# Output product in four strips of 160 columns, mask and memory transposes in 32-column strips, token values one segment later

## The chip, the cores and the metric

The kernel runs on one core of one Trainium2 chip. The metric is the device time of one execution in microseconds (us). An execution uses TensorE (matrix products; its weight loads are listed apart as PEld), VectorE (DVE), ScalarE (ACT), GpSimd (POOL) and the queue of SyncE (SP), which starts most transfers.

## The reference

A pre-normalised attention block with a small recurrent memory, followed by a feed-forward block, over S = 2048 tokens of width D = 640:

```python
for s in range(n_seg):                       # 64 segments of 32 tokens
    h = concat([mem, x_norm[s*32:(s+1)*32]])  # 8 memory rows + 32 token rows = 40
    q, k, v = h@Wq, h@Wk, h@Wv                # 32 heads of 128
    p = softmax(where(mask, q@k.T * scale, -1e9))
    o = (p@v) @ Wo                            # 40 x 640
    mem = o[:8]                               # the next segment's memory
    outs.append(o[8:])
h  = x + concat(outs)
h2 = h + relu(layernorm(h)@w1 + b1)**2 @ w2 + b2      # F = 1728
```

`x_norm` is the layer norm of x. A memory row sees all 40 columns; a token row sees the 8 memory columns and the tokens up to itself. All is bf16. The memory makes the 64 segments a chain: a segment's q, k and v need the output rows of the segment before.

## The kernel before, in words

**Tiling.** The order of every engine's instructions is the order of the program text (a manual schedule); a tile's buffers and the data set the waits. `step(b, sp)` handles segment s = 4b + sp; a block b is four segments, 128 tokens. The 40 rows of a segment are split in three: 8 memory rows and the first 24 token rows (a 32-row operand, `hT4`), and the last 8 token rows, the tail. The tail rows' projections do not depend on the memory, so those of four segments are gathered 32 at a time (`hTt`) and projected a block ahead, as fill work.

**TensorE in strips.** Since an operand has only 32 rows, most products use the array as four strips of 32 columns: four matmuls with different weights' columns run side by side, each writing its own 32 partitions. `proj` (L199) does q, k, v so: 5 contraction chunks * 4 strips of 512 columns for each half n of the heads. `wo_rounds` (L228), the output product, puts two halves of the heads and two halves of the 640 columns on the four strips: 16 rounds of 320 columns; the sums of the two head halves lie on different partitions and `wo_out` adds them (ScalarE copies one half, L233, VectorE adds the other, L235). `o` has 64 rows: two column halves of 320.

**A step** runs in this order on TensorE: q and k of half 0, q and k of half 1 (each evacuated by ScalarE as a row tile, then turned by VectorE, `flip`, L220; GpSimd spreads the memory queries into `qz`, L348 and L350), the memory scores `scores(0)` (L359), v half 0 and two chunks of v half 1, `scores(1)`, the mask product (L426: identity times a mask tile of 8 * 40 columns, which starts the token scores' accumulation), the token scores (L431), the rest of v. The memory rows' softmax (`soft1`, `soft2`) gives `pTm`; `values(0)` and `values(1)` (L389, L393) multiply it with `v` and with the tail values `vt4`; `values_out` (L398) copies the result into `oT`. The token rows' softmax follows on VectorE, ScalarE and GpSimd (`mxk` L439, `tk` L444, `ek` L449, `zk` L455, `rk` L457, `pk` L459, `pkt` L462). Then comes the output product of `oT[:, p, 0:32]`. Its 32 rows are the 8 memory rows of segment s and the 24 token rows of segment s - 1, since the token values of segment s (L484, L489, from `pTk` L470, `pTt` L472 and `pTx` L475) come only after it, and are copied by ScalarE at L496. From the product, `wo_out` gives `o`; `store_main` (L321) writes the token rows of s - 1, and `mem_to_hT` (L293, L297, copy L299) turns the memory rows into the next segment's `hT4`.

**Fill work.** `fill` is a list of small TensorE pieces put into fixed places of the step: 3 pieces after the token softmax's exponential, 2 before the output product, 2 before the memory transposes, the rest behind them. In blocks 1 to 14 a step has 10 pieces (the next block's tail projection: v in the first segment, q in the second, k in the third) or, in the last segment of a block, 8 pieces of the tail output product and a transpose. Blocks 0 and 15 have little or none. `late` and `mid` hold VectorE work of the layer norm at the step's start and before the output product.

**Transfers.** A block's tail values go to DRAM (`vt_d`, L310) and come back in another layout as 16 transfers (L316), four for each group g of 32 partitions. The weights of q, k, v are loaded as four chunks of 128 rows each and one chunk in two pieces of 64 rows (`load_w`, L113; `load_w4`, L118); x, the memory and copies of the mask and of `same` are issued on SP ahead of them (L125, L133, L135, L136). `ffn_biases` (L511, L513, GpSimd copy L515) loads the feed-forward bias seven segments before the end.

**Buffers** that matter: the accumulator tile `po` has one buffer of 4 banks, `chn` (scores, `pw`, `pm`) one bank, the projections three; `o` has two buffers, `v` one.

Of the kernel before, what the change touches and what calls it, by code (L numbers as in the profile page):

```python
# [9 lines left out]
ALU = mybir.AluOpType  # L10
# [6 lines left out]
def kernel(  # L17
# [16 lines left out]
    nc = tc.nc  # L34
# [22 lines left out]
    ROWS = ((0, 128), (DH, 128), (128, 128), (DH + 128, 128))  # L57
# [23 lines left out]
    selg = ident[0:64, 0:64].rearrange("p (g r) -> p g r", r=32)  # L81
    mhalf = const.tile([128, 1], F32)
    nc.vector.memset(mhalf[:], -0.5)
    mask = const.tile([128, HG, NK], BF16)
    nc.vector.memset(mask[0:32], 0.0)
    nc.gpsimd.affine_select(out=mask[0:32], in_=mask[0:32], compare_op=ALU.is_ge, fill=NEG, base=M,
                            pattern=[[0, HG], [-1, NK]], channel_multiplier=1)
# [5 lines left out]
    nc.vector.tensor_copy(out=same[0:32], in_=ident[0:32, 0:32].rearrange("p (j k) -> p j k", k=TL))  # L93
    nc.vector.tensor_reduce(out=diag[0:32], in_=same[0:32], op=ALU.add, axis=AX.X)
    nc.vector.tensor_copy(out=same[0:32], in_=diag[0:32].unsqueeze(2).to_broadcast([32, 4, TL]))
# [13 lines left out]
    def load_w(w, src):  # L109
        w2d = src.rearrange("d h e -> d (h e)")  # L110
        for c in range(4):
            r0, n = ROWS[c]
            nc.sync.dma_start(out=w[:, c * HE:(c + 1) * HE], in_=w2d[r0:r0 + n, :])  # L113

    def load_w4(w, src):
        w2d = src.rearrange("d h e -> d (h e)")
        for ch in range(2):
            (nc.scalar if ch else nc.sync).dma_start(out=w[64 * ch:64 * ch + 64, 4 * HE:5 * HE],  # L118
                                                     in_=w2d[ch * DH + 256:(ch + 1) * DH, :])
# [3 lines left out]
    def load_x(b):  # L123
        xt = s2.tile([128, D], BF16, tag="xt", name="xt")
        nc.sync.dma_start(out=xt[:], in_=x2d[b * 128:(b + 1) * 128, :])  # L125
        xts[b] = xt

    load_x(0)
    load_x(1)
    o0 = s2.tile([64, DH], BF16, tag="o", name="o")  # L130
    nc.vector.memset(o0[:], 0.0)
    for ch in range(2):
        nc.sync.dma_start(out=o0[32 * ch:32 * ch + M, :], in_=A_mem0[0][:, ch * DH:(ch + 1) * DH])  # L133
    for g in range(1, G):
        nc.sync.dma_start(out=mask[32 * g:32 * g + 32], in_=mask[0:32])  # L135
        nc.sync.dma_start(out=same[32 * g:32 * g + 32], in_=same[0:32])  # L136
    for w, src in ((wq, A_Wq), (wk, A_Wk), (wv, A_Wv)):
        load_w4(w, src)
# [26 lines left out]
    def ln_norm(b):  # L165
        mv, rs = xns[b]
        xn = s1.tile([128, D], BF16, tag="xn", name="xn")
        xt = xts.pop(b)
        for d_, s_ in ((xn[:, 0:512].rearrange("p (c g q) -> p c g q", c=2, g=2),
                        xt[:].rearrange("p (g f) -> p g f", g=2)[:, :, 0:256].rearrange("p g (c q) -> p c g q", c=2)),  # L170
                       (xn[:, 512:D].rearrange("p (g q) -> p g q", g=2),
                        xt[:].rearrange("p (g f) -> p g f", g=2)[:, :, 256:DH])):
            nc.vector.tensor_scalar(out=d_, in0=s_, scalar1=mv[:, 0:1], scalar2=rs[:, 0:1],
                                    op0=ALU.subtract, op1=ALU.mult)
        xns[b] = xn

    def ln_transpose(b):
# [5 lines left out]
        hTt = s2.tile([128, DC, 4, TL], BF16, tag="hTt", name="hTt")  # L183
        ptv = pt[:, 0:640].rearrange("p (c s t) -> p c s t", c=DC, s=4)
        nc.scalar.copy(out=hT4[:, :, :, M:SEG], in_=ptv[:, :, :, 0:HD])
        nc.scalar.copy(out=hTt[:], in_=ptv[:, :, :, HD:SEG])
# [35 lines left out]
    def wo_rounds(lhs, pw, h0, h1):  # L222
        for h in range(h0, h1):
            for kh in range(2):
                for ch in range(2):
                    j = kh * 2 + ch
# [499 lines left out]
```

## Time and profile before

| | |
|---|---|
| median of 3 runs | 1091.34 us (1088.5 to 1091.79) |
| the profiled execution | 1091.96 us |
| its span, first to last instruction | 1090.1 us |
| granted TensorE clock | 0.991 |
| TensorE busy | 1015.6 us (93%), 25284 matmuls |
| VectorE, ScalarE, GpSimd busy | 608.5, 532.3, 257.3 us (56%, 49%, 24%) |
| DMA | 38926 packets, 50.81 MB |
| first step's q product to last mask product | 63.2 to 945.8 us |
| feed-forward part | 956.3 to the end |

The span is what the trace covers; the execution's time holds 1.9 us around it. A busy TensorE is not one at its peak: its matmuls are pipelined and their ends modelled, so that times are best read from start to start. The chain that ended last is followed back from the last instruction through what released each step; what is not on it costs nothing unless its cover goes.

### The profile page before, as it was taken

The numbers are of one execution on the slowest core, as the hardware profiler recorded it, in microseconds if no ns is written. First come the engines' busy times: TensorE is split into PE (matmuls) and PEld (weight loads), VectorE is DVE, ScalarE is ACT, GpSimd is POOL, SyncE is SP. The second block draws the span as 40 slices with busy tenths as digits, with TensorE's granted clock in tenths as the row PEclk, the third lists the DMA queues.
The fourth block names the chain that finished last, engine by engine and source line by source line (L and its number), as shares of the span: only waits on it lengthen the run. The fifth ranks groups of instructions, "written<-read, shape, count | busy, mean of one in ns | idle before, by whom it ended". The sixth has DMA issues, their size and how long they took to land.

```text
span 1090.1 us, 56115 instructions
## 1 busy us (share of the span) xinstructions
PE 1015.6 (93%) x25284; PEld 559.4 (51%) x25284; DVE 608.5 (56%) x1735; ACT 532.3 (49%) x1236; POOL 257.3 (24%) x788
## 2 busy tenths in 40 slices
PE   0488999999999999999999999999999699989998
PEld 0144555555555555556555555555555355545555
DVE  1136565656565656565656565656565366555442
ACT  1035555555555555555555555555555255434332
POOL 1002222222222222222222222222222123252220
PEclk9989999999999999999999999999999899999999
DMA  8950000000000000000000000000000110332200
GB/s 227 411 184 15 12 26 13 26 13 26 13 26 13 26 13 25 14 25 13 26 14 25 14 25 14 25 14 25 14 25 8 35 30 21 117 113 73 73 25 25
DMA packets 38926, 50.81 MB, mean 47 GB/s; under 512 B 7472, under 2 KB 34080, under 8 KB 36768
## 3 DMA queue, kind: packets, MB, share of 16 engines
q1 hardware_dynamic: 38448, 45.67, 12.9%
q8 instruction: 198, 3.24, 1.3%
q10 hardware_dynamic: 240, 1.57, 0.6%
q14 instruction: 40, 0.33, 0.1%
HBM read 37.71 MB, written 9.44 MB: 43 GB/s over the span
## 4 chain that ended last, share of the span: by engine, by line
PE 86%; DMA 7%; DVE 2%; SPq 2%; ACT 1%; issue 1%; POOL 0%; DVEq 0%; POOLq 0%; ACTq 0%
PE ps L199 47%; PE pw L228 12%; PE y L679 5%; PE ps L652 5%; PE ps L228 4%; PE po L389 2%; DMA wv<-in_A_Wv_dram 2%; PE ps L431 2%; PE sm L359 2%; DMA wq<-in_A_Wq_dram 2%; PE ps L426 1%; DMA vt_d<-vt 1%; PE po L393 1%; PE pm L293 1%; PE pt L484 1%; PE pt L489 1%
## 5 line engine op out<-in xcount | busy, mean ns | idle before, releaser
L199 PEld LDWEIGHTS <-hT 128*32 128x32 bf16 x7680 | 200.4, 97 | 184.5 <-issue 9.5
L199 PE MATMUL ps<-wk,hT 128*32 128x512 bf16 x2560 | 162.0, 382 | 4.5 <-ACT vt L263 4.5
L199 PE MATMUL ps<-wv,hT 128*32 128x512 bf16 x2560 | 163.7, 383 | 0.0
L199 PE MATMUL ps<-wq,hT 128*32 128x512 bf16 x2560 | 161.6, 381 | 2.1 <-DVE hT L299 2.1
L228 PE MATMUL pw<-wo,oT 128*32 128x320 bf16 x4160 | 153.2, 299 | 1.0 <-ACT oT L496 0.7
L220 DVE STREAM_TRANSPOSE qT<-row 128x512 bf16<-128x512 bf16 x128 | 91.0, 711 | 100.5 <-ACT row L215 100.5
L215 ACT ACTIVATE row<-ps 128x512 bf16<-128x512 f32 x160 | 97.1, 607 | 85.4 <-PE ps L199 84.2
L217 ACT CAST row<-ps 128x512 bf16<-128x512 f32 x160 | 93.8, 586 | 77.1 <-PE ps L199 70.0
L228 PEld LDWEIGHTS <-oT 128*32 128x32 bf16 x4160 | 110.6, 97 | 38.3 <-ACT oT L398 0.9
L459 POOL TENSOR_TENSOR pk<-ek,rk 128x256 bf16<-128x256 bf16 x64 | 39.8, 623 | 309.0 <-DVE rk L457 191.3
L220 DVE STREAM_TRANSPOSE kT<-row 128x512 bf16<-128x512 bf16 x128 | 90.9, 710 | 19.5 <-ACT row L217 18.9
L233 ACT COPY otmp<-pw 64x320 f32<-64x320 f32 x65 | 27.5, 422 | 106.0 <-PE pw L228 106.0
L498 POOL COPY oTt<-oT 128x256 bf16<-128x256 bf16 x64 | 25.5, 398 | 217.4 <-ACT oT L496 217.4
L496 ACT CAST oT<-pt 128x512 bf16<-128x512 f32 x128 | 68.8, 593 | 4.2 <-PE pt L489 3.7
L235 DVE TENSOR_TENSOR o<-pw,otmp 64x320 bf16<-64x320 f32 x65 | 31.4, 483 | 63.2 <-ACT otmp L233 63.1
L199 PEld LDWEIGHTS <-hTt 128*32 128x32 bf16 x1920 | 37.4, 97 | 53.4 <-issue 36.6
L199 PE MATMUL ps<-wq,hTt 128*32 128x512 bf16 x640 | 48.3, 401 | 14.7 <-DMA wq<-in_A_Wq_dram 14.7
L679 PE MATMUL y<-wq,wk 128*128 128x320 bf16 x416 | 61.1, 299 | 0.1
L348 POOL COPY qz<-qT 128x96 bf16<-128x96 bf16 x126 | 33.8, 268 | 114.8 <-DVE qT L220 57.7
L368 ACT ACTIVATE em<-sm,mx 128x40 bf16<-128x40 f32 x126 | 37.5, 297 | 35.8 <-DVE mx L365 35.8
L199 PE MATMUL ps<-wv,hTt 128*32 128x512 bf16 x640 | 47.9, 398 | 6.6 <-DMA wv<-in_A_Wv_dram 6.6
L455 DVE TENSOR_REDUCE zk<-ek 128x8 f32<-128x320 bf16 x64 | 31.1, 486 | 40.0 <-ACT ek L449 40.0
(99 smaller groups left out, 1475.1 us busy)
## 6 DMA issues: line engine op xcount, KB each, us to landing
wo<-in_A_Wo_dram SPq DMA_DIRECT2D x4, 1280.0 KB
wq<-in_A_Wq_dram SPq DMA_DIRECT2D x4, 1024.0 KB
wk<-in_A_Wk_dram SPq DMA_DIRECT2D x4, 1024.0 KB
wv<-in_A_Wv_dram SPq DMA_DIRECT2D x4, 1024.0 KB
vt_d<-vt SPq DMA_DIRECT2D x16, 256.0 KB
vt<-vt_d SPq DMA_DIRECT2D x256, 16.0 KB
xt<-in_A_x_dram SPq DMA_DIRECT2D x16, 160.0 KB
out_dram<-wv SPq DMA_DIRECT2D x16, 160.0 KB
```

The lines of the kernel that those rows point to most:

```text
L199: nc.tensor.matmul(ps[32 * k:32 * k + 32, :], lhsT=lhs(c), rhs=wr[:, c, n, k], start=(c == 0), stop=(c == DC - 1))
L215: nc.scalar.mul(out=row[:], in_=ps[:], mul=scale)
L217: nc.scalar.copy(out=row[:], in_=ps[:])
L220: nc.vector.transpose(out=dst[:, n * 16:(n + 1) * 16, 0:32], in_=row[:].rearrange("p (h e) -> p h e", e=32))
L228: nc.tensor.matmul(pw[32 * j:32 * j + 32, 0:DH], lhsT=lhs(p), rhs=wo[:, head(p), ch * DH:(ch + 1) * DH], start=(h == 0), stop=(h == 15))
L235: nc.vector.tensor_tensor(out=o[:], in0=pw[0:64, 0:DH], in1=tmp[:], op=ALU.add)
L348: nc.gpsimd.tensor_copy(out=d.rearrange("p a (j f) -> p a j f", j=3)[:, :, :, 0:M], in_=src[:, :, 0:3, :])
L368: nc.scalar.activation(out=em[:], in_=sms[n][:, 0:NK], func=ACT.Exp, bias=mx[:, 0:1], scale=1.0, accum_out=zm[:])
L459: nc.gpsimd.tensor_tensor(out=pk[:], in0=ek[:, :, 0:SEG], in1=rk[:].unsqueeze(2).to_broadcast([128, HG, SEG]), op=ALU.mult)
L496: nc.scalar.copy(out=oTg[:, n, :, :, M:NK], in_=po[:, :, n * 128:(n + 1) * 128].rearrange("p g (j q) -> p g j q", q=32))
L652: nc.tensor.matmul(ps[:], lhsT=w1[:, c, fc * 128:(fc + 1) * 128], rhs=hnT[:, c, :], start=(c == 0), stop=(c == DC - 1))
L679: nc.tensor.matmul(y[:, hh, 0:DH], lhsT=f1T[:, fc, k * 128:(k + 1) * 128], rhs=w2[:, fc, cs], start=(fc == 0), stop=False, skip_group_chec ...
```

## The change

It does this, part by part:

- the output product becomes 32 rounds (one per head) of four strips of 160 columns; `o` becomes 128 rows of 160 columns with six buffers, taken out by one VectorE copy; it is stored by four transfers instead of two;
- the contraction index of x, `hT4` and the weights is permuted to match (`q c x` order), so that weights load as five chunks of 128 rows, all on SP, while x and the memory load from ScalarE's queue; the mask and `same` are computed on all partitions instead of being copied there by transfers;
- the mask product becomes four strips of 256 columns (token columns only);
- the memory transposes become 20 matmuls of 32-column shape with 8 columns each;
- the token values of segment s are computed in step s + 1, ahead of the memory values, into the same `po` tile (token columns 0 to 255, memory columns 256 to 319); the token softmax moves behind the memory values; the token rows reach the output product one segment later still, and one more output product runs at the end;
- `mid` moves behind the memory transposes;
- the tail values come back by 4 transfers instead of 16;
- `ffn_biases` moves to the first segment of block 1; the tail output of block 14 runs one segment later.

```diff
-    mask = const.tile([128, HG, NK], BF16)
-    nc.vector.memset(mask[0:32], 0.0)
+    mask = const.tile([128, HG, SEG], BF16)
+    nc.vector.memset(mask[:], 0.0)
...
-        w2d = src.rearrange("d h e -> d (h e)")
-        for c in range(4):
-            r0, n = ROWS[c]
-            nc.sync.dma_start(out=w[:, c * HE:(c + 1) * HE], in_=w2d[r0:r0 + n, :])
+        w2d = src.rearrange("(q c x) h e -> c q x (h e)", q=4, x=32)
+        for c in range(DC):
+            nc.sync.dma_start(out=w[:, c * HE:(c + 1) * HE], in_=w2d[c])
...
+    load_x(0, nc.scalar)
+    load_x(1, nc.scalar)
+    o0 = s2.tile([128, DQ], BF16, tag="o", name="o", bufs=6)
...
-    for g in range(1, G):
-        nc.sync.dma_start(out=mask[32 * g:32 * g + 32], in_=mask[0:32])
-        nc.sync.dma_start(out=same[32 * g:32 * g + 32], in_=same[0:32])
-    for w, src in ((wq, A_Wq), (wk, A_Wk), (wv, A_Wv)):
-        load_w4(w, src)
...
+    def wo_rounds(lhs, pw, p0, p1):
+        for p in range(p0, p1):
+            for q in range(4):
+                nc.tensor.matmul(pw[32 * q:32 * q + 32, 0:DQ], lhsT=lhs(p), rhs=wo[:, head(p), q * DQ:(q + 1) * DQ],
+                                 start=(p == 0), stop=(p == H - 1))
     def wo_out(pw):
-        tmp = s1.tile([64, DH], F32, tag="otmp", name="otmp")
-        nc.scalar.copy(out=tmp[:], in_=pw[64:128, 0:DH])
-        o = s2.tile([64, DH], BF16, tag="o", name="o")
-        nc.vector.tensor_tensor(out=o[:], in0=pw[0:64, 0:DH], in1=tmp[:], op=ALU.add)
+        o = s2.tile([128, DQ], BF16, tag="o", name="o", bufs=6)
+        nc.vector.tensor_copy(out=o[:], in_=pw[:, 0:DQ])
...
+        for c in range(DC):
+            for q in range(4):
+                nc.tensor.matmul(pm[32 * q:32 * q + 32, c * M:(c + 1) * M], lhsT=o[:, c * 32:(c + 1) * 32],
+                                 rhs=ident[:, 32 * q:32 * q + M], start=True, stop=True)
...
         for g in range(G):
-            for j in range(4):
-                r = 32 * g + TL * j
-                nc.sync.dma_start(out=vt4[r:r + TL].rearrange("p s u e -> p s (u e)"), in_=src[g, j])
+            nc.sync.dma_start(out=vt4[32 * g:32 * g + 32].rearrange("p s u e -> p (s u e)"), in_=src[g])
...
+    def token_values(s, v, vt4, po):
+        sp = s % 4
+        pTk, pTx = back.pop()
+        for i in range(HG):
+            for g in range(G):
+                r = slice(32 * g, 32 * g + 32)
+                nc.tensor.matmul(po[:, g, i * 32:(i + 1) * 32], lhsT=v[r, i * E:(i + 1) * E], rhs=pTk[r, i, :],
+                                 start=(i == 0), stop=False, skip_group_check=True)
...
+    def token_out(s, po):
+        for n in range(2):
+            nc.scalar.copy(out=oTg[:, n, :, :, M:NK],
+                           in_=po[:, :, n * 128:(n + 1) * 128].rearrange("p g (j q) -> p g j q", q=32))
+        nc.gpsimd.tensor_copy(out=oTts[s // 4 % 2][:, :, s % 4 * TL:(s % 4 + 1) * TL], in_=oT[:, :, 32:NK])
...
-        nc.tensor.matmul(sk[:, 0:HG * NK], lhsT=ident[:], rhs=mask[:].rearrange("p i k -> p (i k)"),
-                         start=True, stop=False, skip_group_check=True)
+        for g in range(G):
+            nc.tensor.matmul(skv[32 * g:32 * g + 32, :, M:NK], lhsT=ident[:, 0:32], rhs=mask[:],
+                             start=True, stop=False, skip_group_check=True)
...
+        nc.scalar.copy(out=v[:, 512:1024], in_=ps1[:])
+        run(fill, 3)
+        po = pop.tile([128, G, 512], F32, tag="po", name="po")
+        if s:
+            token_values(s - 1, prev["v"], prev["vt4"], po)
+        if not last:
+            for n, pT in ((0, pT0), (1, pT1)):
+                values(n, pT, po)
+                values_out(n, po)
+        run(fill, 2)
...
+        wo_rounds(lambda p: oT[:, p, 0:32], pw, 0, H)
+        if s:
+            token_out(s - 1, po)
+        o = wo_out(pw)
+        if s > 1:
+            store_main(o, s - 2)
+        if not last:
+            run(fill, 2)
+            mem_to_hT(o, hT4s[(s + 1) // 4], (s + 1) % 4)
+            tails_in((s + 1) // 4, (s + 1) % 4)
         run(mid, 2)
+        run(fill, 100)
...
-            if e == 0:
+            if (b, sp) == (1, 0):
                 ffn_biases()
...
+    po = pop.tile([128, G, 512], F32, tag="po", name="po")
+    token_values(NS - 1, prev["v"], prev["vt4"], po)
     pw = chn.tile([128, 512], F32, tag="ch", name="pw")
+    wo_rounds(lambda p: oT[:, p, 0:32], pw, 0, H)
+    token_out(NS - 1, po)
+    store_main(wo_out(pw), NS - 2)
```

## Prediction

> **What bounds the kernel now.** I read the page's chain first, then TensorE's instructions in order of time over two segments of the steady part, then the chain through the start, then the list of waits.
>
> ```profile
> PE 86%; DMA 7%; DVE 2%; SPq 2%; ACT 1%; issue 1%; POOL 0%; DVEq 0%; POOLq 0%; ACTq 0%
> ```
>
> TensorE carries 86% of the chain that ended last. The other engines matter where TensorE waits for them, and nowhere else. The second view is TensorE's own timeline: start, duration, line, tile, tile shape (contract rows * columns), count.
>
> ```profile
> 319.71 0.31 PE L426 MATMUL ps<-mask,ident 128*128 128x320 bf16 x1
> 319.95 0.38 PE L431 MATMUL ps<-kT,qT 128*32 128x40 bf16 x32
> 320.17 0.84 PE L199 MATMUL ps<-wv,hT 128*32 128x512 bf16 x12
> 320.95 0.26 PE L389 MATMUL po<-pTm,v 32*128 32x8 bf16 x16
> 321.06 0.18 PE L393 MATMUL po<-pTm,vt 32*128 32x32 bf16 x4
> 321.17 0.83 PE L199 MATMUL ps<-wk,hTt 128*32 128x512 bf16 x12
> 321.94 0.26 PE L389 MATMUL po<-pTm,v 32*128 32x8 bf16 x16
> 322.05 0.18 PE L393 MATMUL po<-pTm,vt 32*128 32x32 bf16 x4
> 322.16 0.61 PE L199 MATMUL ps<-wk,hTt 128*32 128x512 bf16 x8
> 322.60 2.35 PE L228 MATMUL pw<-wo,oT 128*32 128x320 bf16 x64
> 324.88 0.37 PE L484 MATMUL pt<-pTk,v 32*128 32x32 bf16 x32
> 325.21 0.39 PE L489 MATMUL pt<-pTx,vt 32*128 32x32 bf16 x8
> 325.53 0.61 PE L199 MATMUL ps<-wk,hTt 128*32 128x512 bf16 x8
> 326.08 0.23 PE L293 MATMUL pm<-ident,o 64*64 64x16 bf16 x4
> 326.16 0.17 PE L297 MATMUL pm<-ident,o 64*64 64x8 bf16 x2
> 326.26 0.83 PE L199 MATMUL ps<-wk,hTt 128*32 128x512 bf16 x12
> 326.92 1.25 PE L199 MATMUL ps<-wq,hT 128*32 128x512 bf16 x20
> 328.00 1.25 PE L199 MATMUL ps<-wk,hT 128*32 128x512 bf16 x20
> ...
> 348.27 0.87 PE L393 MATMUL po<-pTm,vt 32*128 32x32 bf16 x4
> ```
>
> Durations overlap, so I read starts only. Four matmuls of one tile shape run side by side; I call that a round. A 512-column round is (328.00 - 326.92) / 5 = 0.216 us. The mask product is one full-width matmul of 320 columns and takes 319.95 - 319.71 = 0.24. The output product takes 324.88 - 322.60 = 2.28 for 16 rounds of 320. Both hold a change of tile shape. With 0.10 us for such a change the output product's round is 0.136 and the mask's 0.14, which agree; so 0.10 is the price of a change of shape, and a round costs 0.0027 + 0.000417 per column (from 512 and 320). Very short rounds have a floor: 32 matmuls of 40 columns take 320.17 - 319.95 = 0.22, or 0.0275 a round, their weight loads included. From one mask product to the next (start to start) a segment lasts 13.44; 13.65 where the tail output runs, about 14.2 in the first segment of a block, about 12.6 in block 0, where no fill work exists.
>
> **Part by part.**
>
> *Mask.* Four strips of 256 columns in the shape of the products around it: one round, 0.109, against 0.24, and the change of shape ahead of it (0.10) goes too. Saved 0.23. If the four ran one after the other it would be 0.43, a loss of 0.1.
>
> *Output product.* 32 rounds of 160 columns: 32 * 0.0694 = 2.22, before 16 * 0.136 = 2.18: +0.04. No row has 160 columns; the loads are hidden at 320 and 512, and the floor of 0.0275 is under 0.069, so I take it as streaming. The far bound is stream plus a whole floor: 0.097 a round. [...] The 320-column rounds, which would have shown that at 0.16 instead of 0.136, speak against it.
>
> *Taking the product out.* ScalarE's copy (L233, 422 ns) and VectorE's sum (L235, 483 ns) become one VectorE copy of 160 columns: between L299 (40 columns, 200 ns) and L439 (320 columns, 491 ns), by straight line 0.32. From the last round's start: matmul 0.23 (by line from 40, 320 and 512 columns: 181, 299, 382 ns), copy 0.32, two handovers 0.06: 0.61. TensorE now has only two fill units to run meanwhile (0.43) plus the round itself (0.07): a new wait of 0.11, where before the token values stood there as cover. Bounds: 0 with a copy of 0.2, 0.28 with 0.49.
>
> *Memory transposes.* Before, 0.10 change of shape + 326.26 - 326.08 = 0.28. After, 20 small matmuls in the ruling shape, 5 rounds at the floor: 0.14. Saved 0.14.
>
> *Token values a segment later.* Now they open the row-tiled block ahead of the memory values. Before: three separate visits to the 32*128 shape: 321.17 - 320.95 + 0.10, 322.16 - 321.94 + 0.10, and 325.53 - 324.88 + 0.10, together 1.39; the last holds two waits of about 0.1 and 0.17 for VectorE and GpSimd (L484 to L489 is 0.33 for eight rounds of 0.0275). After: change in and out 0.2, 20 rounds at 0.0255 (between (0.22 - 0.10) / 5 = 0.024 and the floor of 0.0275), 0.51, no wait for the probabilities, which are a segment old. But memory values 1 now follow memory values 0 at once, into the same accumulator banks that ScalarE is copying out of. The trace never shows TensorE writing a bank being read. What it shows is the same two products in the first segment, when nothing covered them:
>
> ```profile
> 79.08 0.28 ACT oT L398
> ...
> 79.39 0.26 PE po L389 x16
> ```
>
> The matmul before it began at 78.87, so copy and handovers cost 0.5. The new code writes other columns of the same banks; the wait is between 0 (columns told apart) and 0.5 (the row above). I take 0.5, as the nearest row has this same pair. Behind that wait TensorE's whole queue stands, fill and output product included. [...] So 1.39 becomes 0.2 + 0.51 + 0.5 = 1.21; saved 0.18. The second copy (values_out 1) is needed only from output round 17 on, 0.43 + 1.1 later, and is hidden; uncovered it would cost 0.5.
>
> *Softmax of the tokens, moved behind the memory values.* ScalarE's ek now stands after both copies and a fill evacuation (0.59), VectorE's zk and rk end about 2.5 after the second values, the product's end comes at about 2.75 to 2.95. Hidden, narrowly; the rival below prices it. ScalarE's two token copies (1.1) and GpSimd's copies (0.4, 0.4, 0.4, then pTx 0.44) move behind the product and end some 3.2 after it; the next segment's first spread is wanted at 3.8. The layer norm, its strides included, runs behind the transposes on VectorE, off the path.
>
> Sum of a full segment: -0.23 + 0.04 + 0.11 - 0.14 - 0.18 = -0.40; and single first rounds after a change of shape cost 0.01 to 0.02 more than the rest (x8 groups: 0.44 - 0.432 etc.), some eight changes fewer: -0.12. **-0.52**, 42 segments (blocks 1 to 14, three each): **-21.8**.
>
> *First segments of a block.* L393 takes 349.06 - 348.27 = 0.79 there against 0.11 + 0.10 elsewhere in the block: each of its four matmuls has waits on the landings of four value transfers of its own. With one transfer per row group I leave 0.035 for each: 0.55 saved. 14 * (-0.52 - 0.55) = **-15.0**.
>
> *Uncovered segments* (blocks 0 and 15, seven of them, 12.6 where nothing else is in them): there the handover of 0.95 + 0.06 (copy and sum) shrinks to 0.35 and the token softmax (mxk to pTx, on the chain at 90.5 to 95.3) leaves the path. Start to start I add up 4.32 (q and k) + 0.1 + 1.51 + 0.1 + 0.11 + 0.22 + 0.65 + 0.35 + 0.13 + 0.5 + 0.23 + 2.22 + 0.6 + 0.14 + 0.42 = 11.6: -1.0 each against 12.6, and 0.35 more in the two first segments with their transfer waits: **-7.7**.
>
> *Biases.* The wait list has
>
> ```profile
> PE sm L359 <- POOL qz L348: 8.5, 1, 8.5
> ```
>
> GpSimd sat on b1f for 9.6 us until the bias landed, because SP first had to issue sixteen value loads (0.344 each from 850.94 to 856.09). That segment is 24.35 long, its neighbour 14.19. At the new place SP has four stores (0.35), one x load (0.45), the biases (1.9) and the landing (2.4) behind the output: about 6.8 after the product, plus copy and spread 0.7; TensorE asks at 5.5. Left 2.0: **-8.1**. If the wait simply moves whole, 0.
>
> *Start.*
>
> ```profile
> 15.14 16.79 DMA wq<-in_A_Wq_dram
> 31.95 21.37 DMA wv<-in_A_Wv_dram
> ```
>
> Full 128-row weight chunks land every 2.49 (TensorE's waits at 27.00, 29.50, 31.97), but SP issued the first at 13.56, after mask copies that waited for landings; the half-height pieces filled the queues until then. Now 15 chunks start at 0.72: 0.72 + about 2 + 15 * 2.49 + 0.8 for x = 40.9, against 53.3: **-12.4**. The output weights and the first value store follow in the same order, so the 4.5 wait after them moves along. Bounds: 0 (something else holds SP) to -14.
>
> *End.* One more output product, 2.2, and the token values now stand behind the last softmax and the last copy: about +3.9 from the last v to the feed-forward part; the 2.9 wait of L652 on the o buffer goes (six buffers). **+1**. Four stores instead of two per segment add 0.7 on SP, which waits for o anyway.
>
> Together -21.8 - 15.0 - 7.7 - 8.1 - 12.4 + 1 = -64.0. The profiled execution took 1091.96 (span 1090.1, 1.9 around it), 0.6 over the median of the three runs, less than the 0.3% (3 us) that can be told apart here. 1091.96 - 64.0 = **1028**.
>
> **Rivals.**
> *No bank wait.* 63 segments * 0.5 less: 1028 - 31.5 = 997. For: the columns are disjoint. Against: the row at 79.08.
> *The handover gets late.* If VectorE reaches the copy of the product only after rk, or spread falls behind GpSimd's longer tail, each 0.1 costs 6.4; a slip of 0.5 gives 1060, with half the start gain lost as well 1066. For: margins of 0.2 to 0.4. Against: VectorE is busy 56%.
> *Loads exposed (slower).* In the output product each round pays stream plus floor, 0.097 instead of 0.069: 82 products * 32 * 0.0275 = +72: 1100. It decides from 0.094 a round on, where 2624 rounds eat the 64. For: no row has so narrow a product of this kind. Against: 320-column rounds hide their loads whole.
>
> **How the numbers follow.** Forecast 0.58, its own range 1012 to 1046 (bounds of mask, copy, transposes, biases). No bank wait 0.13; late handover 0.22; exposed loads 0.06; gains cancelled to within 0.3% 0.01. The range 996 to 1060 leaves out the upper half of the late cases and the slower one. Faster 0.93, same 0.01, slower 0.06.
>
> **What would show it.** Mask to mask 12.9 in full segments and 13.1 in the first of a block; mask round 0.11; output product 2.22 plus no change of shape behind it; one gap of about 0.5 between the two memory values; a gap near 0.1 ahead of the transposes; first projections of block 0 done near 41. Wrong would be an output product over 3 us, no gap between the memory values, or a start that still ends near 53.

## The result and the profile after

The changed kernel takes **1283.53 us** (median of 4 runs, 1282.05 to 1290.51) against 1090.74 for the kernel before beside it: ratio **1.1783 [1.1736, 1.183]**. The forecast was 1028 with a range of 996 to 1060; it is wrong in size and in sign.

Three stretches of the two profiles, cut at the first and last mask product (TensorE's timeline), say where the 191.3 us of span lie:

| | before | after | difference |
|---|---|---|---|
| start to the first mask product | 76.66 | 185.66 | +109.0 |
| first to last mask product (63 segments) | 869.19 | 942.91 | +73.7 |
| last mask product to the end | 144.2 | 152.8 | +8.6 |

The chain that ended last, of the changed kernel, shares of the span by engine:

```profile
PE 76%; DMA 7%; SPq 7%; issue 7%; ACT 2%; DVE 1%; POOL 0%; DVEq 0%; POOLq 0%; ACTq 0%
```

Two entries have grown: SPq from 2% to 7% (by the page's list of lines it is L113, where SP issues the weight loads) and "issue" from 1% to 7%. "issue" is time in which TensorE waited for nothing that the profile shows. The list of TensorE's waits (us in total, times, longest) says the same by line:

```profile
PE ps L185 <- DMA wv<-in_A_Wv_dram: 50.0, 5, 12.5
...
PE pw L211 <- issue: 33.4, 42, 4.2
PE po L390 <- ACT oT L400: 28.4, 63, 0.7
```

The first row is the start; with those for wk (44.2) and wq (37.3) it makes 131.5 us, against 26.4 for the same three weights before. The last is the bank wait that the forecast priced at 0.5, in every segment. The one between is new, and so are 35 us more of "issue" on L211, L315 and L185.

**The start.** TensorE's timeline (start, duration, what, idle before):

```profile
49.13 0.62 PE L185 MATMUL ps<-wq,hTt 128*32 128x512 bf16 x4 [9.27 <-DMA wq<-in_A_Wq_dram]
```

The same wait before it ends at 39.25: a 1 MB chunk lands every 49.13 - 39.25 = 9.9 us; before, every 2.49. The transfer view for 60 to 140 us of the changed kernel (packets, MB, share of the 16 transfer engines) shows them mostly idle while TensorE waits:

```profile
q1 hardware_dynamic: 1730, 9.14, 30.9%
```

In most slices of that view the rate is 106 GB/s, a quarter of what e1 below reaches.

**The steady part.** TensorE's timeline through one output product, the counterpart of 320.95 to 326.26 before:

```profile
428.19 0.37 PE L310 MATMUL po<-pTk,v 32*128 32x32 bf16 x32
...
429.25 0.26 PE L390 MATMUL po<-pTm,v 32*128 32x8 bf16 x16 [0.43 <-ACT oT L400]
...
429.91 1.49 PE L211 MATMUL pw<-wo,oT 128*32 128x160 bf16 x75
432.09 1.14 PE L211 MATMUL pw<-wo,oT 128*32 128x160 bf16 x53 [0.69 <-issue]
433.00 0.66 PE L185 MATMUL ps<-wv,hTt 128*32 128x512 bf16 x8
433.65 0.29 PE L274 MATMUL pm<-ident,o 128*32 128x8 bf16 x20
```

The product stops after 75 of its 128 matmuls, waits for nothing, and goes on at 432.09. What TensorE lacks there is its next instructions. The trace lists their transfers as a queue of its own; its total (packets, MB, share) on the page of before, then on that of the changed kernel:

```profile
q8 instruction: 198, 3.24, 1.3%
...
q8 instruction: 248, 4.06, 1.3%
```

A packet holds 16384 bytes, and 248 of them fit TensorE's 31676 matmuls and 31684 weight loads at 256 instructions a packet (63360 / 256 = 247.5). Beside TensorE's stops, in the records of single packets:

```
packet landed   411.13   415.04   418.52   430.86
TensorE goes on 412.66   416.49   419.95   432.09
```

Over the steady part of the changed kernel 92 stops end in this way, 1.39 us (median; 1.17 to 1.60) after a packet has landed, and they sum to 77.0 us. Before there were 2, together 0.4. (The list of waits, which counts idle time alone, has 71.6 us of "issue" for the changed kernel's steady part; sums of stops here and below are good to some 6 us.) Between the stops that ended at 416.49 and 419.95 TensorE issued exactly 256 instructions. The same holds from the start of the trace on. At 77 of the 78 stops of over 0.3 us, and at all 101 in e3 below, the matmuls and loads run so far, divided by 256, give the number of packets landed so far, and in e3 the remainder falls evenly from 186 to 125. So a stop comes where TensorE has used up what has landed. In no run did two of these packets land closer together than 3.2 us (3.23 before, 3.25 in the changed kernel), so 256 / 3.2 = 80 instructions a us is the most that was ever delivered. The stretch above, to the next fill work at 433.79, has 244 matmuls with 244 loads in 433.79 - 428.19 = 5.6 us, 4.9 without the stop: 100 a us asked for. The kernel before has 178 and 178 in 5.3 us: 67.

### The profile page after: what moved, and what is told of

It is laid out like the page before. It is cut to its first block, busy times and chain, and to the rows that moved or that the text cites. A ratio compares the mean times of both kernels' runs of the same rounds, so it can differ in the third digit from the quotient of the medians.

```text
span 1281.4 us, 68779 instructions
## 1 busy us (share of the span) xinstructions
PE 1007.4 (79%) x31676; PEld 651.8 (51%) x31684; DVE 590.3 (46%) x1723; ACT 520.7 (41%) x1155; POOL 258.4 (20%) x788
## 3 DMA queue, kind: packets, MB, share of 16 engines
q1 hardware_dynamic: 41820, 46.83, 11.6%
## 4 chain that ended last, share of the span: by engine, by line
PE 76%; DMA 7%; SPq 7%; issue 7%; ACT 2%; DVE 1%; POOL 0%; DVEq 0%; POOLq 0%; ACTq 0%
PE ps L185 40%; PE pw L211 13%; SPq L113 7%; PE y L678 4%; PE ps L651 4%; DMA wv<-in_A_Wv_dram 4%; PE ps L211 3%; DMA wq<-in_A_Wq_dram 2%; PE po L390 2%; PE sm L360 2%; PE po L310 2%; ACT oT L400 1%; PE pm L274 1%; PE ps L436 1%; PE po L395 1%
## 5 line engine op out<-in xcount | busy, mean ns | idle before, releaser
L185 PEld LDWEIGHTS <-hT 128*32 128x32 bf16 x7680 | 226.0, 97 | 158.4 <-issue 11.1
L211 PE MATMUL pw<-wo,oT 128*32 128x160 bf16 x8448 | 184.7, 245 | 34.5 <-issue 33.4
L211 PEld LDWEIGHTS <-oT 128*32 128x32 bf16 x8448 | 166.5, 103 | 53.5 <-issue 45.7
L185 PE MATMUL ps<-wk,hT 128*32 128x512 bf16 x2560 | 166.0, 382 | 3.5 <-ACT vt L244 3.5
L185 PE MATMUL ps<-wq,hT 128*32 128x512 bf16 x2560 | 166.4, 383 | 2.4 <-DVE hT L276 2.3
L185 PE MATMUL ps<-wv,hT 128*32 128x512 bf16 x2560 | 163.1, 379 | 0.0
L185 PEld LDWEIGHTS <-hTt 128*32 128x32 bf16 x1920 | 47.8, 98 | 179.5 <-issue 151.7
L320 ACT CAST oT<-po 128x512 bf16<-128x512 f32 x128 | 74.9, 585 | 107.2 <-PE pw L211 102.1
L465 POOL TENSOR_TENSOR pkt<-ek,rk 128x64 bf16<-128x64 bf16 x64 | 18.9, 295 | 434.1 <-DVE rk L463 352.8
L185 PE MATMUL ps<-wq,hTt 128*32 128x512 bf16 x640 | 53.6, 406 | 47.5 <-DMA wq<-in_A_Wq_dram 37.3
L185 PE MATMUL ps<-wv,hTt 128*32 128x512 bf16 x640 | 48.4, 395 | 50.0 <-DMA wv<-in_A_Wv_dram 50.0
L349 POOL COPY qz<-qT 128x96 bf16<-128x96 bf16 x126 | 33.4, 265 | 258.2 <-DVE qT L206 184.1
L185 PE MATMUL ps<-wk,hTt 128*32 128x512 bf16 x640 | 48.0, 395 | 44.2 <-DMA wk<-in_A_Wk_dram 44.2
L400 ACT CAST oT<-po 128x128 bf16<-128x128 f32 x126 | 33.5, 266 | 89.6 <-PE po L395 89.5
L216 DVE CAST o<-pw 128x160 bf16<-128x160 f32 x66 | 21.4, 325 | 101.2 <-PE pw L211 101.2
L206 DVE STREAM_TRANSPOSE qTt<-row 128x512 bf16<-128x512 bf16 x32 | 20.6, 676 | 100.6 <-ACT row L201 100.6
L211 PE MATMUL ps<-wo,oTt 128*32 128x160 bf16 x2048 | 50.9, 236 | 14.1 <-issue 13.8
```

The costliest lines, as they stand in the source:

```text
L185: nc.tensor.matmul(ps[32 * k:32 * k + 32, :], lhsT=lhs(c), rhs=wr[:, c, n, k], start=(c == 0), stop=(c == DC - 1))
L206: nc.vector.transpose(out=dst[:, n * 16:(n + 1) * 16, 0:32], in_=row[:].rearrange("p (h e) -> p h e", e=32))
L211: nc.tensor.matmul(pw[32 * q:32 * q + 32, 0:DQ], lhsT=lhs(p), rhs=wo[:, head(p), q * DQ:(q + 1) * DQ], start=(p == 0), stop=(p == H - 1))
L320: nc.scalar.copy(out=oTg[:, n, :, :, M:NK], in_=po[:, :, n * 128:(n + 1) * 128].rearrange("p g (j q) -> p g j q", q=32))
L349: nc.gpsimd.tensor_copy(out=d.rearrange("p a (j f) -> p a j f", j=3)[:, :, :, 0:M], in_=src[:, :, 0:3, :])
L400: nc.scalar.copy(out=oTg[:, n, :, :, 0:M], in_=po[:, :, c0:c0 + 4 * M].rearrange("p g (j m) -> p g j m", m=M))
```

## The experiments

The theory: the start is lost because a weight chunk's source is now cut in four (`c q x`, outermost 4) and keeps only a share of 0.25 of the 16 transfer engines busy (62 to 134 us of the changed kernel, 106 GB/s), and the steady part because the split product needs instructions faster than they arrive. Its rival is the slower one of the prediction: the narrow rounds pay their weight loads and the new waits cost more than the parts saved. Gaps below are TensorE's stops that end 1.1 to 1.7 us after an instruction packet. "Densest 4 us" is the number of TensorE instructions in 4 us that 1% of the steady part's 4 us stretches exceed, divided by 4; it can lie above 80, by what had landed ahead. Each ratio is to the kernel before in the same batch of runs (medians 1090.74 to 1092.26); first mask, steady part, gaps and density are of the one profiled execution.

| kernel | median us | ratio to before | first mask | steady part | gaps, us | densest 4 us, per us |
|---|---|---|---|---|---|---|
| before | 1090.74 | | 76.66 | 869.19 | 0.4 | 76 |
| after | 1283.53 | 1.1783 [1.1736, 1.183] | 185.66 | 942.91 | 77.0 | 100 |
| e1 plain rows | 1158.95 | 1.0611 [1.058, 1.0643] | 65.07 | 935.82 | 72.5 | 102 |
| e4 eight pieces | 1235.44 | 1.1326 [1.127, 1.1382] | 120.45 | 956.50 | 77.1 | 100 |
| e2 half the product's instructions | 1188.73 | 1.0894 [1.0862, 1.0927] | 185.75 | 854.86 | 13.0 | 89 |
| e3 copies later | 1277.31 | 1.1709 [1.1671, 1.1747] | 186.71 | 935.09 | 102.6 | 107 |
| b1 split product on before | 1191.23 | 1.0916 [1.0881, 1.0951] | 76.65 | 964.03 | 75.7 | 100 |
| b2 as many, spread, on before | 1111.14 | 1.0185 [1.0156, 1.0214] | 76.36 | 885.89 | 13.2 | 88 |
| c2 = e1 + e2 + e3 | 1051.63 | 0.9637 [0.9614, 0.966] | 66.13 | 835.57 | 25.9 | 94 |
| v1 | 1140.07 | 1.0448 [1.042, 1.0476] | 78.29 | 908.88 | 28.3 | 95 |
| v2 | 1087.76 | 0.9948 [0.9924, 0.9972] | 65.12 | 874.79 | 32.4 | 96 |
| v3 | 1087.2 | 0.9965 [0.9953, 0.9977] | 64.90 | 874.52 | 25.9 | 95 |
| v4 | 1066.67 | 0.9771 [0.9748, 0.9794] | 65.93 | 855.18 | 3.5 | 82 |

### e1: the same chunks from plain rows

```diff
-        w2d = src.rearrange("(q c x) h e -> c q x (h e)", q=4, x=32)
+        w2d = src.rearrange("(c r) h e -> c r (h e)", r=128)
```

> The changed kernel, with the q, k and v weights loaded as five plain chunks of 128 consecutive rows (the rows' permutation is left out, so the products pair rows that do not belong together). Same bytes, same 15 transfers, same queue. Theory (the shape of the source decides the rate): in the changed kernel a chunk takes 9.55 us from landing to landing, in the kernel before 2.49; with plain rows the chunks land every 2.5 again, the first mask product comes near 70 instead of 185.7, and the time falls by 105 to 115, to about 1173. Rival (SP or the other queue holds the chunks back): the chunks still land every 9.5 and the time stays within 10 of 1283.

The first mask product comes at 65.07, 120.6 us earlier than in the changed kernel and 11.6 earlier than before. The transfer view for 20 to 40 us of this run:

```profile
DMA packets 1154, 8.41 MB, mean 421 GB/s; under 512 B 128, under 2 KB 128, under 8 KB 128
q1 hardware_dynamic: 1153, 8.40, 101.0%
```

Chunks of the same bytes, 26.42 - 23.95 = 2.47 apart by TensorE's waits, and all engines busy. The edit touches nothing else of the transfers, so the whole loss of the start is the form of the source. The time fell by 124.6, somewhat more than the 105 to 115 expected. The steady part keeps its 72.5 us of gaps: the two losses are separate.

### e4: the outer dimension eight instead of four

```diff
-        w2d = src.rearrange("(q c x) h e -> c q x (h e)", q=4, x=32)
+        w2d = src.rearrange("(q c x) h e -> c q x (h e)", q=8, x=16)
```

> The changed kernel, with the weights' 128 rows of a chunk taken as 8 pieces of 16 rows instead of 4 pieces of 32 (the pairing of the rows is then left out). Theory (a transfer of this kind keeps only as many packets in flight as its outer dimension has pieces: 4 of 16 engines busy in the changed kernel, 25%): 8 in flight, about 212 GB/s, a chunk every 4.8 us; the first mask product near 115 instead of 185.7, the time near 1212. Rival (any source in three dimensions runs at about 106 GB/s): a chunk still takes 9.5, the time stays near 1283.

The transfer view for 40 to 70 us:

```profile
DMA packets 810, 6.09 MB, mean 203 GB/s; under 512 B 44, under 2 KB 72, under 8 KB 72
q1 hardware_dynamic: 809, 6.07, 51.7%
```

TensorE's waits for chunks end at 52.74 and 57.73. Four pieces 9.9 us a chunk at 106 GB/s, eight 5.0 at 203, whole rows 2.47 at 421: from four pieces to eight the rate doubled. The busy share of the transfer engines did too: 0.25 in the changed kernel (two tenths in most slices of its view, where the last slices raise the mean to 30.9%), 51.7% here, against 101.0% with whole rows. The time, 1235.44 over two runs, misses the 1212 expected by 23 us: the first chunks took 6.0 to 6.7 us each, so that the first mask product came at 120.45 instead of 115, and the steady part was 13.6 us longer than the changed kernel's, for a reason that stays open.

### e2: half the product's instructions

```diff
-        for p in range(p0, p1):
+        for p in range(p0, p1, 2):
             for q in range(4):
-                nc.tensor.matmul(pw[32*q:32*q+32, 0:DQ], lhsT=lhs(p), rhs=wo[:, head(p), q*DQ:(q+1)*DQ], ...)
+                nc.tensor.matmul(pw[32*q:32*q+32, 0:DH], lhsT=lhs(p + q//2),
+                                 rhs=wo[:, head(p + q//2), q%2*DH:(q%2+1)*DH], ...)
```

> The changed kernel, with the output product as 16 rounds of 320 columns: the two halves of the heads land on different partitions and only 160 of each 320 columns are taken on, so the sum of the head halves is left out. The columns that TensorE streams per product are the same (16 * 320 = 32 * 160); the matmuls and weight loads are halved, 64 pairs fewer per segment and 64 fewer per tail product. Theory (TensorE runs out of instructions): the gaps that end about 1.4 us after an instruction packet has landed (92 of them, about 77 us) disappear almost wholly, and the time falls by 70 to 100, to 1185 to 1215. Rival (160-column rounds are slow by themselves, their loads exposed): rounds would be longer inside a product, not between; a product's continuous stretch is 0.069 a round already, so the gain would be under 10.

The columns streamed are the same, in 64 matmuls instead of 128. The steady part is 88.1 us shorter than the changed kernel's and its gaps shrink from 77.0 to 13.0. The timeline of the same stretch:

```profile
617.59 0.29 PE L391 MATMUL po<-pTm,v 32*128 32x8 bf16 x16
...
618.37 0.26 PE L391 MATMUL po<-pTm,v 32*128 32x8 bf16 x16 [0.43 <-ACT oT L401]
...
619.04 2.39 PE L211 MATMUL pw<-wo,oT 128*32 128x320 bf16 x64
621.21 0.65 PE L185 MATMUL ps<-wv,hTt 128*32 128x512 bf16 x8
621.84 0.29 PE L275 MATMUL pm<-ident,o 128*32 128x8 bf16 x20
```

The product is whole (621.21 - 619.04 = 2.17) and the forecast's other waits now stand free: 617.59 to 618.37 is 0.78 for a group that takes 608.15 - 607.99 = 0.16 where nothing holds it (c2), a bank wait of 0.62; 621.21 to 621.84 is 0.63 for two fill rounds of 0.43, a handover wait of 0.20. The gain of 94.8 is within the 70 to 100 expected, but the gaps did not go "almost wholly".

### e3: both copies out behind both products

```diff
-                values(n, pT, po)
-                values_out(n, po)
+                values(n, pT, po)
+            for n in range(2):
+                values_out(n, po)
```

> The changed kernel, with ScalarE's two copies of the memory values both put behind the second memory values product, so that no copy reads the accumulator banks while TensorE has still to write them. In the changed kernel TensorE waits 0.45 for the first copy in each of 63 segments. Theory (bank wait, freely additive): -28, to 1255. Theory (TensorE also short of instructions): the wait let instructions gather, so only a part comes back: -8 to -22, with the gaps after instruction packets growing by the rest. Rival (the wait was for something else, such as the probabilities of half 1): no change, and the gap between the two products stays.

This takes the bank wait away, 28.4 us by the list of the changed kernel. The steady part shortens by 7.8 only, since the gaps grow from 77.0 to 102.6. From the list of waits:

```profile
PE pw L211 <- issue: 53.4, 56, 3.5
```

In the changed kernel this row has 33.4. The time went from one wait into the other: instructions land while TensorE stands at the banks (in the changed kernel a packet lands at 922.01, within the wait of 0.43 us that ends at 922.35). The gain of 6.2 in all lies just under the smaller of the two forecasts.

### b1: only the product's split, in the kernel before

```diff
-            for kh in range(2):
-                for ch in range(2):
-                    ... pw[..., 0:DH] ... wo[:, head(p), ch * DH:(ch + 1) * DH]
+            for c0 in (0, 160):
+                for j in range(4):
+                    ... pw[..., c0:c0 + 160] ... wo[:, head(p), ch * DH + c0:ch * DH + c0 + 160]
```

> The kernel before, with only this changed: each 320-column matmul of the output product is split into two of 160 columns with the same weights loaded twice. The result is the same, the streamed columns too; 64 more matmul and load pairs per segment and 64 per tail product. Theory (TensorE runs out of instructions): 888 instead of 760 TensorE instructions in a full segment and some 1020 in the last of a block, at no more than about 78 per us: little or nothing in the first three segments of a block (0 to 0.7 each), +1 to +3 in the last, gaps ending about 1.4 us after a packet: +30 to +80 in all, 1120 to 1170. Rival (short rounds cost only their stream): +0.04 per product, +3 in all.

One edit costs 99 us, more than the 30 to 80 expected of it. TensorE's timeline:

```profile
603.95 2.31 PE L228 MATMUL pw<-wo,oT 128*32 128x160 bf16 x123
607.33 0.30 PE L228 MATMUL pw<-wo,oT 128*32 128x160 bf16 x5 [1.07 <-issue]
```

Up to the stop, the 123 matmuls start within 2.08 us, 0.068 a round: they stream as forecast. Gaps make 75.3 of the steady part's +94.8. Its steady part also holds six windows of 3.4 us and one of 10.2 at half clock, 30.7 us in all, against one of 10.2 before; if they cost up to half their length where they fall on the path, an estimate from their lengths, that is up to 10 us more than before. How much of the rest they are was not tried.

### b2: as many instructions, elsewhere

```diff
+        if cut:
+            for c in range(c0, c1):
+                for z in range(2):
+                    for k in range(4):
+                        ... ps[..., z * 256:z * 256 + 256] ... wr[:, c, n, k, 2 * z:2 * z + 2]
```

Used in the kernel before for q and for v, whose 512-column rounds become pairs of 256.

> The kernel before, with 80 more matmul and load pairs per segment, the same mean number that splitting the output product adds (64 + 64 / 4), but in other places: the q and v projections of the segment are cut into matmuls of 256 columns, spread over two thirds of the segment. Theory A (a mean rate binds: 920 instructions need 920 / 78 = 11.8 us, less than a segment's 13.4): nothing but the 0.0027 per extra round, 20 * 64 * 0.0027 = +3.5, and few gaps; 1094 to 1103. Theory B (the store of fetched instructions is short, so any stretch that uses them faster than one packet per 3.3 us starves): 8 instructions per 0.11 us is 73 per us, just under the rate, but the short products behind it then start with an empty store: +20 to +60, with the gaps in the short products. Rival (any extra instruction costs the same wherever it stands): +99.

238 instruction packets, nearly b1's 239, and the loss is +20 instead of +99: 13.2 us of gaps. That is the low end of theory B, though only part of the stops lie in the short products; theory A and the rival miss it. Here not the number of instructions counts but how many a stretch asks for in a few us: a split q asks 80 in 1.08 us (74 a us), the split output product 256 in 2.2 (115 a us).

### c2: e1, e2 and e3 together

> The changed kernel with plain weight rows, the output product in 16 rounds of 320 columns without the sum of the head halves, and both value copies behind both products: the three single edits in one. If their gains add, 1283.5 - 124.6 - 94.8 - 6.2 = 1058. With instructions no longer short, the copies' edit should give its whole 28 instead of 6: 1036. If the forecast's other terms had been right, the sum without the bank wait would be 997 + 1 to 5 here; what lies above that is the sum of the mis-sized terms.

1051.63, between the 1058 of gains that add and the 1036 of a bank wait that comes back whole. With e1's and e2's edits it is no replacement, but it shows that the change's other parts, in e3's order of copies, do save time: the steady part is 33.6 shorter than before, a segment without a gap takes 12.68 from mask to mask against 13.44. 25.9 us of gaps are left, more than e2's 13.0; the stretch is denser without the bank wait (94 a us against 89).

### v1 to v4: a complete version

v1 keeps the new order of the work (token values in step s + 1, token softmax behind the memory values, mask in strips, four value transfers) with the old output product, `wo_out`, transposes and loads, and has e3's order of copies.

> A kernel that computes everything: the changed kernel's order (token values a segment later, mask in strips of 256, softmax of the tokens behind the memory values, biases early, four tail value transfers), with the output product in 16 rounds of 320, its two-part evacuation, the six-matmul memory transposes and the row layout of the kernel before, and both value copies behind both products. TensorE instructions per segment about 766 against 760 before. Forecast from the terms that the runs showed: full segments 13.44 - 0.23 - 0.7 (token values without their waits) + 0.3 (the longer handover, three fill units ahead of it) = about 12.8, first segments 1.0 less than before, last ones 13.1; steady part 869 - 45, biases included in it -8, start between 0 and -10: 1030 to 1050. Rival (instructions run short again, since the token and memory values now follow each other): gaps at the output product, 1050 to 1090.

1140.07; the forecast was wrong. From its list of waits:

```profile
PE pm L290 <- DVE o L232: 64.5, 63, 2.1
```

63 waits of about 1.0 us for `o`. `wo_out` starts with a ScalarE copy, and v1 issued `token_out`'s two ScalarE copies ahead of it, as the changed kernel does, where it costs nothing because `wo_out` is VectorE's alone.

v2 puts `o = wo_out(pw)` ahead of `token_out`, loads plain rows as five chunks, turns the memory with ten matmuls of 64 * 64, and gives the fill places 2, 2, 4, 2 pieces.

> The combined kernel again, computing everything, with three edits: the product is taken out ahead of ScalarE's token copies (in the combined kernel ScalarE's 1.1 of token copies stood ahead of its half of the evacuation, and the transposes waited 1.01 in 63 segments, 64.5 in all); weights in five plain chunks of 128 rows with ten 64-row memory transposes to match; fill units 2, 2, 4, 2 instead of 3, 2, 3, 2. Forecast: 1140 - 60 (the wait; 0.95 of handover against 0.86 of fill) - 13 (first mask product at 65 instead of 78) = 1067; a segment of about 12.75; with fewer gaps after instruction packets 1050. Rival (with the wait gone, instructions run short as they did when the bank wait was taken out): gaps grow from 28 to over 60, 1090 or more.

1087.76 over 12 runs, with a spread of 1077.46 to 1094.74: the start is 11.5 better, but the steady part is 5.6 longer than before, with 32.4 us of gaps. Its timeline:

```profile
177.72 0.18 PE L393 MATMUL po<-pTm,v 32*128 32x8 bf16 x4 [1.04 <-issue]
```

Its output product has 64 matmuls; the token and memory values just ahead of it, 80 small matmuls that take 162.75 - 162.01 = 0.74 us where nothing stops them, ask for the rest. The forecast of 1067 was missed; its rival has the time nearly right (1090 or more) but not the gaps, 32.4 us instead of over 60.

v3 differs in the fill (3, 2, 3, 2).

> The same, with fill units 3, 2, 3, 2. The handover of 0.95 then stands against 0.65 of fill in the blocks that have it: 0.2 to 0.3 more waiting ahead of the transposes per segment, +12 to +18 against the version with 4 there, unless the wait lets instructions gather and gives it back: then within 6 of it.

The same time, as the second half of the expectation has it: the waits for `o` (L277) grow from 13.8 to 26.9 us, and the gaps shrink to 25.9. Where the fill stands around the stretch does not settle it.

v4 takes the token values out of the stretch. They need only the segment before, so they can stand among q and k (the fill places are 3, 1, 4, 2):

```diff
+        po = pop.tile([128, G, 512], F32, tag="po", name="po")
+        if s:
+            token_values(s - 1, prev["v"], prev["vt4"], po)
         # k of half 1 follows here
...
-        run(fill, 2)
-        po = pop.tile([128, G, 512], F32, tag="po", name="po")
-        if s:
-            token_values(s - 1, prev["v"], prev["vt4"], po)
+        run(fill, 3)
```

> The mended combined kernel with the same instructions in another place: the token values of the segment before stand between q and k of half 1, among 512-column rounds, instead of directly ahead of the memory values; fill units 3, 1, 4, 2. Theory (what counts is how many instructions follow each other in little time, not their number): the stretch of scores, token values and memory values, about 300 instructions in 2.3 us, falls apart; of the 36 gaps (32 us) after instruction packets, 21 us of them at the memory values, most disappear, and with them the 3.4 us at half clock that follow the longest; the two more changes of shape cost 0.2 a segment, 13: 1088 - 32 - 10 + 13 = about 1058. Rival (the mean number of instructions binds): no fewer gaps, and the 13 are lost: 1100.

**1066.67** against the 1058 expected, ratio 0.9771 [0.9748, 0.9794]: faster than both kernels. Its timeline has the moved work between q at 600.69 and k at 602.26, whose 512-column rounds ask 20 matmuls in 1.08 us (with the loads, 37 instructions a us):

```profile
601.88 0.37 PE L313 MATMUL po<-pTk,v 32*128 32x32 bf16 x32
```

Gaps fall from 32.4 (v2) to 3.5 us. The longest of its waits in the steady part:

```profile
PE pm L277 <- DVE o L218: 14.2, 49, 1.0
```

Of its 22.2 us in the span, 10.7 come from the start and 14.0 from the steady part (the end gives 2.5 back). The largest wait left is the 14.2 for `o`.

**Against the rival.** In e2, c2 and the unbroken parts of the changed kernel the steady part shows no large wait but the priced ones and the stops, and rounds of 160 columns stream at the forecast speed (next section). The theory stands: e1 and e4 for the start; for the steady part e2, b1 and b2, and the order of the table (by a measure picked after the runs), in which gaps are small up to 82 a us, 13 us at 88 and 89, 26 to 32 at 94 to 96, and 72 to 103 from 100 on.

## Why the prediction was wrong, point by point

**Start: the step that failed** is "Now 15 chunks start at 0.72: 0.72 + about 2 + 15 * 2.49". The 2.49 was the price of a chunk of plain rows, used for a chunk whose source is cut in four. With plain rows the step is right: e1 gains 11.6 where 12.4 was forecast. As written it lost 109.0, so the term was off by 121. No weight chunk of before had a source of this form; the bounds "0 to -14" assumed the rate and only doubted the order.

**Steady part: the step that failed** is "The loads are hidden at 320 and 512, and the floor of 0.0275 is under 0.069, so I take it as streaming". As streaming it is right: 17.5 rounds of the changed kernel ran in 400.97 - 399.78 = 1.19, 0.068 a round against 0.0694 forecast. What it left out is that 64 more matmuls and 64 more loads per product must be fetched. The trace of before shows the fetch: 198 packets in 1090.1 us, 5.5 us apart on average, and single packets 3.2 us apart. The product alone wants one packet's worth in 2.2 us. So the term for the supply of instructions stood at nothing, and the stops that it makes measured 77.0 us.

The other terms, by their rows:

- *Mask*: 0.11 a round forecast, 615.66 - 615.55 = 0.11 in e2. Right.
- *Transposes*: 0.14 forecast, 433.79 - 433.65 = 0.14. Right.
- *Bank wait*: 0.5 forecast, 0.62 in e2; the changed kernel has it in all 63 segments. Right in kind; the rival without it is out.
- *Handover*: 0.11 forecast; 0.17 (0.60 for two fill rounds of 0.43) in most segments of e2 and c2 without a stop there, 0.29 at most. Mis-sized by 0.06 to 0.2.
- *Full segment*: -0.52 forecast; in e2 13.44 - 13.17 = -0.27, and the two terms above are most of the difference of 0.25 (0.12 + 0.09 by the rows under e2). *First segment of a block*: 13.1 forecast, 13.17 in e2.
- *Uncovered segments*: 11.6 forecast; e2's in block 0 take 11.83, 12.57 and 11.95. Somewhat short.
- *Biases*: 2.0 left forecast. The changed kernel's list of waits has 1.5, so 7.0 of the 8.5 went (the segment of 24.35 also held the 10.2 us at half clock, from 855.85 on):

```profile
PE sm L360 <- POOL qz L349: 1.5, 1, 1.5
```

- *End*: +1 forecast, +8.6 measured. The last step's product stops for instructions for 4.24 us and the product after it for 1.79, the first of them here (TensorE's timeline):

```profile
1135.63 3.06 PE L211 MATMUL pw<-wo,oT 128*32 128x160 bf16 x85 [4.24 <-issue]
```

The feed-forward weights load at that time, and the transfer engines are busy throughout (a share of 1.01 from 1130 to 1136). That the two compete for them fits, but was not tried.

From the forecast -52.6 for the steady part (21.8 + 15.0 + 7.7 + 8.1) to the measured +73.7 are 126.3 us. The gaps are 76.6 of them, half-clock windows up to 12 (34.1 us against 10.2 before, half of the difference), bank and handover wait 13 (63 * 0.21). Some 25 us are not placed. Nor does the forecast come out without the split: e2's steady part gains 14.3 of the 52.6, with 13.0 of gaps and those 13 of waits, and 12 are open.

**The rivals.** "Loads exposed (slower)" had the right sign and, for the steady part, nearly the right size (+72 on 1028), but not its mechanism: the rounds were not at 0.097, the time lies in stops between them. Its chance of 0.06 was worked out for that mechanism alone; the supply of instructions, and the form of a source, were no rivals at all. Both had something to be read from: the diff gives the instructions per us of each stretch, and the new source pattern is a form of which the trace of before has no row of that size. "Wrong would be an output product over 3 us ... or a start that still ends near 53" named the right places: the product of 429.91 lasts until 433.00, 3.1 us, and the start ends later still.

## What to carry to other kernels

When an edit splits TensorE instructions at equal columns, count instructions per us in the densest few us and set them against the spacing of the instruction packets in the trace: here 256 in 3.2 us at best. Cure a dense stretch by moving small matmuls among wide ones: here a wait removed inside it mostly turned into other stops (e3), while moving 40 of its 80 small matmuls away took the gaps from 32.4 to 3.5 us (v2 to v4). Price a transfer by a row with the same outer dimensions, not by its bytes: the same 1 MB took 2.47, 5.0 or 9.9 us.

## What the runs showed of the hardware

- A stretch of slow rounds did not keep TensorE from stopping behind it. In the changed kernel packets land at 402.07, 405.80 and 411.13: the slow rounds of q and k stand there, 20 matmuls in 1.08 us, and the last packet comes 5.33 us after the one before, where the closest two of this trace lie 3.25 apart; at 410.97 TensorE then stops. An estimate of what was held, from the records of single packets and with the end of a block of 256 read from the stops: 427 (the changed kernel), 476 (b2), 489 (e3) and 513 (b1) instructions at most were landed and not yet run when a packet landed in the steady part, so up to about two packets' worth.
- Behind some of the stops the granted clock was 0.50 for 3.4 us. The changed kernel's timeline just behind a stop of 1.32 us that ended at 246.23 (the releaser is "issue"), and its busy times in that window (stretch, length, busy PE, PEld, DVE, ACT, POOL with counts, then the granted clock, DMA share and GB/s):

```profile
247.64 4.11 PE L211 MATMUL pw<-wo,oT 128*32 128x160 bf16 x128
251.51 0.66 PE L185 MATMUL ps<-wv,hTt 128*32 128x512 bf16 x8
```

```profile
246.30:251.50 5.20, 4.78 (x176) 4.31 (x179) 0.69 (x2) 2.07 (x5) 0.87 (x2) 0.67 0.02 6
```

  After the stop come 3.4 us at half clock (0.67 on average over this window; 1.00 in the 10 us before): the product took 251.51 - 247.64 = 3.87 instead of 2.2, 1.7 us more behind a stop of 1.32. Ten such windows lie in the changed kernel's steady part, one in v4's. In the 3.4 us ahead of each of the ten TensorE was idle for 1.36 to 1.79 us, a share of 0.40 to 0.52; in eight of these stretches a stop and a bank wait both end. e3, with 102.6 us of gaps and no bank wait, has three windows. That the idle time brings the window about is read from their order in time, not shown by a run of its own.
- The bank wait hid a shortage of instructions here: e3 removed 28.4 us of it and gained 7.8 in the steady part, while the gaps grew from 77.0 to 102.6.
